# Two-layer decode attention: K scored in the step that transposes it, two more K slots kept, no self-waits on the tensor engine

## The chip, the core and the metric

The kernel runs on one core of a Trainium2 chip. The core has five engines that each work through a list of instructions in order: PE (matrix products), DVE (vector operations), ACT (activations and copies), POOL (here sums over partitions) and SP, which here only starts transfers (DMA). They meet at semaphores. The metric is the time of one execution in microseconds (us), as median of several runs.

## The reference

Two blocks, attention and a small feed-forward network, are applied twice to a batch of eight single tokens; both passes use the same caches and weights.

```python
B, Sq, D = 8, 1, 512;  Hq, Hkv, Sk, Dh = 32, 8, 8192, 128;  F = 1792     # bf16
def _A_ref(x, k_cache, v_cache, wq, wo):     # k_cache, v_cache [8, 8, 8192, 128]
    q = (x @ wq) split into 32 heads; four query heads share one K/V head
    p = _softmax(q @ k^T * Dh ** -0.5)
    return (p @ v, heads joined) @ wo
def _B_ref(x, w1, w2): return _silu(x @ w1) @ w2
x = x + _A_ref(_layernorm(x), ...);  x = x + _B_ref(_layernorm(x), ...)   # layer 0
x = x + _A_ref(_layernorm(x), ...);  x = x + _B_ref(_layernorm(x), ...)   # layer 1
```

K and V together are 268 MB, and both layers need all of them, so the kernel is mostly a stream of K and V into the core.

## The kernel before

**Tasks and positions.** A task is one K/V head of one batch row in one layer: 2 x 8 x 8 = 128 tasks. It has four granules (loads of 512 KB for K and as many for V), each of two halves; a half is a position, so a task has eight positions, whose number modulo 8 is called its phase here. Two positions, one granule, are called a step. The loop over `p` writes out the order of the work for every engine by hand.

**Slots.** Loads go into 27 slots of an arena. A K granule is transposed by PE (eight 128x128 transposes per half, `emit_t`, T below), and the result is copied from PSUM back to its own slot by ACT or DVE (ACT takes three copies of eight). Then `emit_s` (S) multiplies it with the queries: four products of 128x512 per granule. `emit_pv` (PV) multiplies V with the probabilities, `LP` = 14 positions later; eight products per half. `plan_loads` gives each load the slot that comes free earliest in planned order, and SP issues the loads in that order, each as soon as the last readers of its slot are done.

**Kept K.** Of the 32 K granules of a row the last `KEEP` = 18 stay in their slots, transposed, from layer 0 to layer 1: heads 4 to 7, and two of the four granules of head 3. Layer 1 then loads only V for them. `make_tasks` orders the tasks so that a row's kept heads run in layer 0, then a few tasks of other rows, then the same heads in layer 1 (the "kept tasks"). In the tasks between these two stretches, 27 - 18 = 9 slots are left for the stream.

**Order within a step.** `emit_t_until(p + LT)` with `LT` = 2 writes T one step ahead of S. At an odd `p` come S of this granule, then the PV of two halves, then at some phases a part of the softmax (`soft`: at phase 0 row maximum and spread on DVE; at 2 the shift, a small product on PE, then own and shift on DVE, then exp on ACT; at 4 a sum; at 5 the transposes of P and their copy on DVE; at 7 a reciprocal).

**Chains.** When a row's layer 0 attention is done, the small work that leads to its layer 1 query is cut into stages (`chain_of`), and one stage is written per position after the softmax part: residual sum ("attended"), three stages of a layer norm, two empty ones, two halves of w1, silu, an empty one, two halves of w2, a second norm of three stages, two empty ones, four quarters of wq. A norm's third stage is thirteen short DVE operations. For rows 1 to 6 the first norm's third stage falls on phase 2 of a task and the second's on phase 5; for rows 0 and 7 one position later. The chain ends just ahead of that row's kept tasks. Outside chains a head's share of the wo product (`add_heads`) is written at phase 7, as the output of a head gets ready.

**Waits.** `acquire` makes an engine wait for the last writer of all that an operation reads, and for the last writer and all readers of what it writes, its own earlier operations included.

Lines: copies 436 (ACT) and 438 (DVE), transposes 430, S 461, PV 534, shift 482, P transposes 510, projections 603, wo 621, norm 556 to 590; issues of loads 331.

Of the kernel before, what the change touches and what calls it, by code (L numbers as in the profile page):

```python
# [13 lines left out]
GPT = 8  # L14
GPG = 2
NSLOT = 27
KEEP = 18
LT = 2
PRE = 10
LP = 14  # L20
EARLY = 4
# [8 lines left out]
PVN = 12  # L30
CW = 32
SETTLE = 2
ACT_EVAC = (1, 4, 7)

BF16 = mybir.dt.bfloat16
FP32 = mybir.dt.float32
# [24 lines left out]
class Sync:  # L61
# [30 lines left out]
    def acquire(self, eng, reads=(), writes=()):  # L92
        toks = []
        for r in reads:
            if r.last_write is not None:
                toks.append(r.last_write)
        for r in writes:
            if r.last_write is not None:
                toks.append(r.last_write)
            toks.extend(r.reads)  # L100
        best = {}
        for t in toks:
            k = t.sem
            if k not in best or best[k].val < t.val:
                best[k] = t
        for t in best.values():
            self.wait(eng, t)

    def release(self, tok, reads=(), writes=()):
        for r in reads:  # L110
# [27 lines left out]
def make_tasks(nb, nkv, keep_from):  # L138


    first = int(keep_from)
    a = [[(0, b, g) for g in range(first)] for b in range(nb)]
    kept = [[(0, b, g) for g in range(first, nkv)] for b in range(nb)]
    c = [[(1, b, g) for g in range(first, nkv)] for b in range(nb)]
    d = [[(1, b, g) for g in range(first)] for b in range(nb)]
    ahead = [t for b in range(1, nb) for t in a[b]]
    behind = []
    tasks = a[0] + kept[0]
    na = 0
    for b in range(nb):  # L150
        if b:
            tasks += kept[b]
        size = -(-(2 * first * (nb - 1)) // nb) if b in (0, nb - 1) else 2 * first * (nb - 1) // nb
        must = max(0, first * min(b + 1, nb - 1) - na)
        nd = size if b == nb - 1 else min(len(behind), first, size - must)
        tasks += behind[:nd]
        del behind[:nd]
        take = ahead[na:na + size - nd]
        na += len(take)
        tasks += take  # L160
        if b + 1 == nb:
            tasks += behind
        tasks += c[b]
        behind += d[b]
    assert na == len(ahead)
    return tasks + d[nb - 1]


def plan_loads(tasks, kept, nslot, ngran):
# [3 lines left out]
    for i, (layer, b, g) in enumerate(tasks):  # L173
        for k in range(ngran):
            i0 = i * GPT + k * GPG
            if layer == 0 or (g, k) not in kept:
                need = -1 if i0 < PRE else i0 - LT
                last = i if layer or (g, k) not in kept else at[(1, b, g)]
# [28 lines left out]
def _build(ctx, nc, A_x, A_k_cache, A_v_cache, A_wq, A_wo, B_w1, B_w2, out):  # L207
# [12 lines left out]
    order = [(g, k) for g in range(HKV) for k in range(NGRAN)]  # L220
    kept = set(order[len(order) - KEEP:])
    tasks = make_tasks(B, HKV, (len(order) - KEEP) // NGRAN)
    assert len(tasks) == 2 * B * HKV
    task_at = {t: i for i, t in enumerate(tasks)}
    loads = plan_loads(tasks, kept, NSLOT, NGRAN)
    NG = len(tasks) * GPT
# [9 lines left out]
    def sb(shape, dt, name):  # L236
        _cnt[0] += 1
        return ctx.enter_context(nc.sbuf_tensor(f"{name}_{_cnt[0]}", shape, dt))
# [8 lines left out]
    def chunk(slot, c):  # L247
        o = slot * SLOT + c * 128
        return ARENA[:, o:o + 128]

    def half(slot, h):
        o = slot * SLOT + h * GRP * 128
        return ARENA[:, o:o + GRP * 128]
# [36 lines left out]
    own = sb([128, NQ * USED], FP32, "own")  # L290
# [23 lines left out]
    def r_half(slot, h):  # L314
        return res(f"slot{slot}_{h}")
# [19 lines left out]
    def mm_group(steps, reads=(), writes=()):  # L335
        def run():
            inst = None
            for f in steps:
                inst = f()
            return inst  # L340
        return op(pe, run, reads, writes)
# [14 lines left out]
    with nc.Block() as block:  # L356

        @block.sync
        def _(sync_eng):
# [47 lines left out]
            load_rest()  # L407

            evacs = [0]
            tevacs = [0]  # L410
            tnext = [0]

            def has_t(i):
# [3 lines left out]
            def where(i):  # L417
                _l, b, g = tasks[i // GPT]
                return b, g, (i % GPT) // GPG, i % GPG

            def emit_t(i):
                b, g, k, h = where(i)
                slot = k_slot[(b, g, k)]
                n = tevacs[0]
                tevacs[0] += 1
                tb = evacs[0] % NTP
                evacs[0] += 1
                tpv = TPp[tb][:, :].rearrange("p (k q) -> p k q", q=128)
                steps = [
                    lambda c=c: pe.transpose(tpv[:, c, :], chunk(slot, h * GRP + c), ident[:, :])  # L430
                    for c in range(GRP)
                ]
                mm_group(steps, reads=[r_half(slot, h), "ident"], writes=[f"TP{tb}"])
                dst = half(slot, h)
                if n % 8 in ACT_EVAC:
                    op(act, lambda: act.copy(dst, TPp[tb][:, :]), reads=[f"TP{tb}"], writes=[r_half(slot, h)])  # L436
                else:
                    op(dve, lambda: dve.tensor_copy(dst, TPp[tb][:, :]), reads=[f"TP{tb}"], writes=[r_half(slot, h)])  # L438

            def emit_t_until(i):  # L440
                while tnext[0] <= min(i, NG - 1):
                    if has_t(tnext[0]):
                        emit_t(tnext[0])
                    tnext[0] += 1
# [10 lines left out]
            def emit_s(i):  # L455
                ti = i // GPT
                b, g, k, _h = where(i)
                slot = k_slot[(b, g, k)]
                bank, qn = ti % NSCP, ti % NQB
                steps = [  # L460
                    lambda c=c: pe.matmul(  # L461
                        SCp[bank][c * QUAD:(c + 1) * QUAD, :], QB[qn][:, NGRAN - 1 - k:NGRAN - 1 - k + QUAD],
                        ARENA[:, slot * SLOT + c * KB:slot * SLOT + (c + 1) * KB],
                        start=(k == 0), stop=(k == NGRAN - 1),
                    )
                    for c in range(NQ)
                ]
                mm_group(steps, reads=[r_half(slot, 0), r_half(slot, 1), f"QB{qn}"], writes=[f"SC{bank}"])
# [230 lines left out]
            def add_heads(b):  # L699
                g = heads[b].pop(0)  # L700
                summed[b] += 1
                first, last = summed[b] == 1, summed[b] == HKV
                if b < B:
                    a = at1[b % 3]
                    wo_part(g, lambda h: a[:, h:h + 1], f"at1_{b % 3}", 1, first, last)
                else:
                    wo_part(g, lambda h: at2[:, h, :], "at2", B, first, last)
# [30 lines left out]
            for p in range(NG + LP + GPT + 1):  # L738
                tq = (p + LQ) // GPT
                if (p + LQ) % GPT == 0 and tq < ntask:  # L740
                    layer, b, _g = tasks[tq]
                    if layer == 1 and chain and chain_b[0] == b:
                        while chain:
                            chain.pop(0)()
                    emit_q(tq)
                emit_t_until(p + LT)
                if p % GPG == GPG - 1:
                    if p < NG:
                        emit_s(p)
                    for i in range(p - LP - GPG + 1, p - LP + 1):  # L750
                        if 0 <= i < NG:
                            emit_pv(i)
                ti, ph = p // GPT - 1, p % GPT
                if 0 <= ti < ntask and ph in soft:
                    for f in soft[ph]:
                        f(ti)
                if chain:
                    left = max(1, first1[chain_b[0]] - EARLY - p)
                    for _n in range(-(-len(chain) // left)):
                        chain.pop(0)()  # L760
                elif heads[turn[0]] and not (p < NG and tasks[p // GPT][0] and (tasks[p // GPT][2], 0) in kept
                                             and turn[0] < B):
                    add_heads(turn[0])
                done = p - LP - GPT
                if done >= 0 and done % GPT == 0 and done // GPT < ntask:
                    tj = done // GPT
                    emit_norm(tj)
                    layer, b, _g = tasks[tj]
                    if layer == 0:
                        heads[b].append(_g)  # L770
                    elif b == B - 1:
                        heads[B].append(_g)
                    if layer == 0 and tj == last0[b]:
                        assert not chain and turn[0] == b
                        chain.extend([lambda b=b: add_heads(b)] * (HKV - summed[b]) + chain_of(b))
                        chain_b[0] = b
                        turn[0] = b + 1
                issue_until(p)
# [48 lines left out]
```

## Time and profile before

| | |
|---|---|
| median of 3 runs | 1216.23 us (1215.27 to 1217.24) |
| profiled execution, its own time | 1213.55 us |
| span of its instructions | 1211.5 us |
| busy: PE, weight loads, DVE, ACT | 87%, 65%, 50%, 32% of the span |
| DMA | 473.51 MB on the load queue, 391 GB/s of reads over the span |
| loads of K, of V | 368, 512, each 512 KB |
| copies of transposed K: DVE, ACT | 460 of 688 ns, 276 of 1010 ns |

A line of a timeline gives start, duration, engine, source line, operation, output and inputs, count, and in brackets the idle time before it and what ended it. A line of windows gives the stretch, its length, then each engine's busy time, the granted PE clock, the DMA share and the rate. Ends of PE instructions are modelled, so PE is best read from start to start.

### The profile page before, as it was taken

Reading aid. Unit: us, or ns where it says so; the run is one execution under the profiler, and the core shown is the slowest. Engines: PE = TensorE matmul, PEld = TensorE weight load, DVE = VectorE, ACT = ScalarE, POOL = GpSimd, SP = SyncE. Lnnn points to the kernel's source line nnn. Section 1 sums busy time; section 2 is a strip of 40 time slices with the busy share of each in tenths; the row PEclk is TensorE's granted clock in tenths of the full one; section 3 lists DMA queues with packets and bytes.
Section 4 is the critical chain, followed back from the end, with each engine's and each line's share of the span. In section 5 each row is a group of like instructions: output and inputs, shape, how many; then the busy total and the mean of one; then the engine's idle time right before and its main releaser. Section 6 shows DMA issues by size and latency. Waiting matters only on the chain.

```text
span 1211.5 us, 46232 instructions
## 1 busy us (share of the span) xinstructions
PE 1049.8 (87%) x20216; PEld 793.0 (65%) x20216; DVE 609.6 (50%) x1853; ACT 385.4 (32%) x670; POOL 70.3 (6%) x172
## 2 busy tenths in 40 slices
PE   2698898888898899889888899889998899888985
PEld 2576775666666676667666676667666766667664
DVE  2454554546444554546454554546455554455453
ACT  1233332333233322333233332333233323333231
POOL 0000000000000000000000000000000000000000
PEclk9899999999999999999999999999999999999996
DMA  9999999999999999999999999999999999999994
GB/s 376 384 397 407 406 366 409 408 408 401 352 408 408 408 383 403 408 408 404 367 408 408 407 390 407 408 407 402 386 407 408 406 396 409 408 408 385 399 407 163
DMA packets 133927, 476.45 MB, mean 393 GB/s; under 512 B 14160, under 2 KB 20064, under 8 KB 133216
## 3 DMA queue, kind: packets, MB, share of 16 engines
q1 hardware_dynamic: 133728, 473.51, 99.1%
q8 instruction: 160, 2.62, 0.9%
q14 instruction: 39, 0.32, 0.1%
HBM read 473.44 MB, written 0.01 MB: 391 GB/s over the span
## 4 chain that ended last, share of the span: by engine, by line
DMA 46%; PE 38%; DVE 7%; SPq 5%; issue 3%; ACT 0%; POOL 0%; POOLq 0%; DVEq 0%
DMA arena<-in_A_k_cache_dram 43%; PE OTp L534 14%; PE TPp L430 10%; PE SCp L461 6%; SPq L331 5%; PE MISC L603 4%; DMA wo<-in_A_wo_dram 2%; DVE arena L438 2%; PE OTp L482 1%; DMA arena<-in_A_v_cache_dram 1%; PE TPp L510 1%; PE MISC L621 1%; DVE PT L514 1%; DVE rowmax L472 1%; DVE tr L586 1%
## 5 line engine op out<-in xcount | busy, mean ns | idle before, releaser
L438 DVE COPY arena<-TPp 128x1024 bf16<-128x1024 bf16 x460 | 316.3, 688 | 328.1 <-PE TPp L430 327.9
L430 PE MATMUL TPp<-ident,arena 128*128 128x128 bf16 x5888 | 417.0, 222 | 69.9 <-DMA arena<-in_A_k_cache_dram 54.0
L436 ACT COPY arena<-TPp 128x1024 bf16<-128x1024 bf16 x276 | 278.9, 1010 | 520.1 <-PE TPp L430 520.1
L534 PE MATMUL OTp<-PT,arena 128*128 128x48 bf16 x8192 | 383.1, 185 | 45.8 <-DMA arena<-in_A_v_cache_dram 6.7
L534 PEld LDWEIGHTS OTp<-PT,arena 128*128 128x128 bf16 x8192 | 273.8, 96 | 219.3 <-issue 87.5
L430 PEld LDWEIGHTS TPp<-ident,arena 128*128 128x128 bf16 x5888 | 345.9, 99 | 98.9 <-DMA arena<-in_A_k_cache_dram 79.4
L461 PE MATMUL SCp<-arena,QB 128*32 128x512 bf16 x2048 | 207.3, 394 | 8.5 <-DVE arena L438 5.0
L492 ACT ACTIVATE P<-SCp,shift 128x512 bf16<-128x512 f32 x128 | 88.2, 689 | 257.3 <-PE OTp L534 134.7
L501 POOL PARTITION_ALL_REDUCE ssa<-ssm x128 | 55.4, 433 | 998.6 <-DVE ssm L498 968.8
L461 PEld LDWEIGHTS SCp<-arena,QB 128*32 128x32 bf16 x2048 | 53.1, 93 | 58.4 <-DVE arena L438 6.4
L472 DVE TENSOR_REDUCE rowmax<-SCp 128x1 f32<-128x512 f32 x128 | 86.9, 679 | 0.0
L514 DVE COPY PT<-TPp 128x256 bf16<-128x256 bf16 x128 | 37.2, 291 | 86.6 <-PE TPp L510 86.6
L485 DVE SCALAR_TENSOR_TENSOR own<-OTp,real,far 128x64 f32<-128x64 f32 x128 | 35.9, 281 | 74.6 <-PE OTp L482 74.4
L482 PE MATMUL OTp<-spread,ones 128*128 128x64 f32 x256 | 51.2, 282 | 1.8 <-DVE spread L474 1.8
L621 PE MATMUL MISC<-at,wo 128*128 128x32 bf16 (+1 forms) x1152 | 40.5, 176 | 11.2 <-DMA wo<-in_A_wo_dram 7.7
L510 PE MATMUL TPp<-ident,P 128*128 128x128 bf16 x512 | 49.2, 218 | 0.0
L498 DVE TENSOR_SCALAR ssm<-hm,rs 128x4 f32<-128x4 f32 x128 | 28.5, 223 | 36.5 <-ACT P L492 36.5
L621 PEld LDWEIGHTS MISC<-at,wo 128*128 128x128 bf16 x1152 | 34.6, 96 | 11.8 <-DMA wo<-in_A_wo_dram 7.8
L482 PEld LDWEIGHTS OTp<-spread,ones 128*128 128x128 f32 x256 | 38.8, 192 | 3.0 <-DVE spread L474 3.0
L603 PE MATMUL MISC<-xnT,wq 128*128 128x32 bf16 (+1 forms) x1152 | 34.6, 176 | 4.5 <-issue 3.0
L603 PEld LDWEIGHTS MISC<-xnT,wq 128*128 128x128 bf16 x1152 | 32.3, 96 | 5.8 <-issue 3.3
L474 DVE TENSOR_SCALAR spread<-ident,rowmax 128x64 f32<-128x64 bf16 x128 | 32.6, 254 | 4.6
(47 smaller groups left out, 293.4 us busy)
## 6 DMA issues: line engine op xcount, KB each, us to landing
arena<-in_A_v_cache_dram SPq DMA_DIRECT2D x512, 512.0 KB, 10.2
arena<-in_A_k_cache_dram SPq DMA_DIRECT2D x368, 512.0 KB, 14.9
wq<-in_A_wq_dram SPq DMA_DIRECT2D x1, 4096.0 KB, 15.8
wo<-in_A_wo_dram SPq DMA_DIRECT2D x1, 4096.0 KB, 26.0
w<-in_B_w_dram SPq DMA_DIRECT2D x2, 1792.0 KB, 22.6
P<-in_A_x_dram SPq DMA_DIRECT2D x1, 8.0 KB
out_dram<-P SPq DMA_DIRECT2D x1, 8.0 KB
```

Of the source, the lines that this page charges most:

```text
L331: eng.dma_start(out_ap, in_ap).then_inc(counter.sem, 16)
L430: lambda c=c: pe.transpose(tpv[:, c, :], chunk(slot, h * GRP + c), ident[:, :])
L436: op(act, lambda: act.copy(dst, TPp[tb][:, :]), reads=[f"TP{tb}"], writes=[r_half(slot, h)])
L438: op(dve, lambda: dve.tensor_copy(dst, TPp[tb][:, :]), reads=[f"TP{tb}"], writes=[r_half(slot, h)])
L461: lambda c=c: pe.matmul(SCp[bank][c * QUAD:(c + 1) * QUAD, :], QB[qn][:, NGRAN - 1 - k:NGRAN - 1 - k + QUAD], ARENA[:, slot * SLOT + c * K ...
L472: op(dve, lambda: dve.tensor_reduce(rowmax[:, :], SCp[bank][:, :], AX.X, ALU.max), reads=[f"SC{bank}"], writes=["rowmax"])
L482: mm_group([lambda: pe.matmul(every, ones[:, :], spread[:, :], start=True, stop=True)], reads=["ones", "spread"], writes=[f"OT{ob}"])
L492: op(act, lambda: act.activation(P[:, :], SCp[bank][:, :], ACT.Exp, bias=shift[:, 0:1], scale=SM_SCALE, accum_out=rs[st][:, :]), reads=[f" ...
L510: lambda c=c: pe.transpose(tpv[:, c, :], P[:, c * 128:(c + 1) * 128], ident[:, :])
L534: lambda c=c, cc=cc: pe.matmul(otp, chunk(slot, h * GRP + c), pv[:, cc % CPB, cc // CPB % NQ, k, :].unsqueeze(2).to_broadcast([128, REP, P ...
L603: lambda o=o, k=k: pe.matmul(MISC[:, o * n:o * n + w], w_sb[:, k, o * 128:(o + 1) * 128], rhs_of(k).to_broadcast([128, w]) if n == 1 else ...
L621: lambda o=o, h=h: pe.matmul(MISC[:, o * w:(o + 1) * w], wo_sb[:, h, o * 128:(o + 1) * 128], rhs_of(h).to_broadcast([128, w]) if n == 1 el ...
```

## The change

`KEEP` goes from 18 to 20: five whole heads (3 to 7) keep their K, so 16 loads of K fewer are made, and seven slots are left to the stream between. The order of the tasks is the same. `LT` goes from 2 to 0, and S is written at the end of its step: a step is now T of half 0, T of half 1, PV of two halves, softmax part, chain stage or wo, S. Half 0 is always copied by ACT and half 1 by DVE. PE no longer waits for its own earlier operations.

```diff
-KEEP = 18
-LT = 2
+KEEP = 20
+LT = 0
-ACT_EVAC = (1, 4, 7)
...
+        own = self.eng_sem[self.nc.tensor.engine]
         for t in best.values():
-            self.wait(eng, t)
+            if t.sem is not own or eng is not self.nc.tensor:
+                self.wait(eng, t)
...
-                if n % 8 in ACT_EVAC:
+                if h == 0:
                     op(act, lambda: act.copy(dst, TPp[tb][:, :]), reads=[f"TP{tb}"], writes=[r_half(slot, h)])
                 else:
                     op(dve, lambda: dve.tensor_copy(dst, TPp[tb][:, :]), reads=[f"TP{tb}"], writes=[r_half(slot, h)])
...
                 emit_t_until(p + LT)
                 if p % GPG == GPG - 1:
-                    if p < NG:
-                        emit_s(p)
                     for i in range(p - LP - GPG + 1, p - LP + 1):
                         if 0 <= i < NG:
                             emit_pv(i)
...
                     add_heads(turn[0])
+                if p < NG and p % GPG == GPG - 1:
+                    emit_s(p)
                 done = p - LP - GPT
```

More of the change, by code (lines that the diff above doesn't have):

```diff
@@ L409, in _ @@
             evacs = [0]
-            tevacs = [0]
             tnext = [0]
@@ L423, in emit_t @@
                 slot = k_slot[(b, g, k)]
-                n = tevacs[0]
-                tevacs[0] += 1
                 tb = evacs[0] % NTP
```

## The prediction

> **What bounds the kernel now.** I read the page first: the DMA row, the GB/s in slices and the chain that ended last.
>
> ```profile
> span 1211.5 us, 46232 instructions
> GB/s 376 384 397 407 406 366 409 408 408 401 352 408 408 408 383 403 408 408 404 367 408 408 407 390 407 408 407 402 386 407 408 406 396 409 408 408 385 399 407 163
> DMA 46%; PE 38%; DVE 7%; SPq 5%; issue 3%; ACT 0%; POOL 0%; POOLq 0%; DVEq 0%
> ```
>
> The stream runs at a ceiling of 408 GB/s, with one dip in each eighth of the span. 473.5 MB at 408 GB/s are 1160 us; the last 18 us have no loads; the rest is start and dips. Windows laid around the flat part and around the dips of batch rows 1 to 6:
>
> ```profile
> 200.00:280.00 80.00, 69.27 (x1245) 51.78 (x1244) 38.81 (x101) 28.50 (x46) 3.44 (x8) 1.00 1.03 407
> ...
> 284.00:324.00 40.00, 35.15 (x794) 27.87 (x791) 21.71 (x80) 12.46 (x22) 2.54 (x6) 1.00 0.96 361
> 428.00:460.00 32.00, 29.99 (x670) 23.50 (x666) 17.70 (x59) 8.62 (x16) 2.10 (x5) 1.00 0.99 379
> 562.00:592.00 30.00, 26.37 (x580) 20.54 (x579) 15.79 (x55) 9.58 (x16) 2.09 (x5) 1.00 0.94 362
> 698.00:726.00 28.00, 26.23 (x583) 20.59 (x580) 16.56 (x56) 8.59 (x15) 2.10 (x5) 1.00 1.01 388
> 832.00:860.00 28.00, 25.33 (x553) 19.87 (x549) 14.35 (x52) 8.57 (x15) 2.10 (x5) 1.00 0.99 377
> 964.00:992.00 28.00, 26.11 (x586) 20.95 (x586) 16.19 (x53) 9.30 (x16) 1.68 (x5) 1.00 1.01 396
> ```
>
> The last number is GB/s. Length times (1 - GB/s / 408) gives the lost time: 4.6, 2.3, 3.4, 1.4, 2.1 and 0.8 us, mean 2.4. Each lies where a row's chain of small stages (norm, projections) is mixed into the last three tasks before that row's kept heads. In between the kernel is bound by loads, in the dips by the PE. The DMA view, asked for a flat stretch (404 to 424 us) and for a dip (444 to 452 us), gives the time from issue to landing:
>
> ```profile
> arena<-in_A_k_cache_dram SPq DMA_DIRECT2D x8, 512.0 KB, 8.5
> arena<-in_A_v_cache_dram SPq DMA_DIRECT2D x7, 512.0 KB, 9.0
> ...
> arena<-in_A_v_cache_dram SPq DMA_DIRECT2D x6, 512.0 KB, 5.6
> ```
>
> A load every 0.524 MB / 408 GB/s = 1.285 us; nine streaming slots make a cycle of 11.6 us, of which 8.75 are on the way and 2.8 are held by compute and the issue. When the PE falls late the 8.75 shrinks, and at 5.6 the rate has already fallen (352 GB/s): the cushion is about 3 us. Last, the timeline: PE and copies in a flat step, DVE in a chain, and an idle PE near the end.
>
> ```profile
> 379.13 1.07 PE L430 MATMUL TPp<-ident,arena 128*128 128x128 bf16 x16 [0.18 <-DMA arena<-in_A_k_cache_dram]
> 379.79 0.69 DVE L438 COPY arena<-TPp 128x1024 bf16<-128x1024 bf16 x1 [1.17 <-PE TPp L430]
> 380.13 0.40 PE L461 MATMUL SCp<-arena,QB 128*32 128x512 bf16 x4
> 380.24 1.01 ACT L436 COPY arena<-TPp 128x1024 bf16<-128x1024 bf16 x1 [1.20 <-PE TPp L430]
> 380.46 0.81 PE L534 MATMUL OTp<-PT,arena 128*128 128x48 bf16 x16
> ...
> 284.10 0.14 DVE L578 TENSOR_SCALAR vr<-s1a 128x1 f32<-128x1 f32 x1
> 286.39 0.18 DVE L590 TENSOR_TENSOR xnT<-xc,yr 128x4 bf16<-128x4 f32 x1
> 286.47 0.69 DVE L438 COPY arena<-TPp 128x1024 bf16<-128x1024 bf16 x1
> ...
> 1181.91 1.03 PE L430 MATMUL TPp<-ident,arena 128*128 128x128 bf16 x8 [1.52 <-DMA arena<-in_A_k_cache_dram]
> ```
>
> Start to start, a step (two positions) is T 1.00, S 0.33, PV 0.65: 1.98 us, under the 2.57 that its two loads take. The first copy starts 0.66 and the second 1.11 after the first transpose. The third stage of a norm holds DVE 2.47 us (284.10 to 286.57 with 11 operations between), and a copy waits behind it.
>
> **The change, part by part.** Sixteen K loads (two per row) and their 256 transposes go. The loads are on the path: 16 x 1.285 = **-20.6 us**. The PE's 16 x 1.00 us lie at the edge of the kept tasks, see below.
>
> *Fewer slots, scored sooner.* K was held over two steps: landing to the end of S in the next step, 2.57 + 1.00 + 0.40 = 4.0 us, V 0.75. Now K is held T 1.0, PV 0.5, S 0.4 and the wait for the copy: 2.4, V about 0.9, since V lands 1.285 after K and its slot is passed on with K's. The mean hold falls by 0.7 us, to 2.1; seven slots cycle in 9.0 us, so 6.9 are left on the way instead of 8.75: the cushion loses **1.9 us in each chain**. SP issues in order behind S, now the last PE group of the step; that is in the hold. Against it, the kept tasks now begin without transposes: two slots come free per 0.9 instead of 2.0 us, and the dip ends earlier, which I take at 0.9. Net +1.0 per chain.
>
> *Self-waits.* PV's second half waited for its first: the waits view has 512 such waits, 85.7 us, 0.17 each. PV becomes 0.48, I take 0.5. Other own waits were long done: 0.
>
> *S behind the copies.* Copy h1 (DVE) runs from 1.11 to 1.80 after the step's start; with 0.1 for the semaphore S starts at 1.9, where T and PV end at 1.5. A plain step is 1.9 + 0.33 = 2.23 us, still under 2.57; the four steps of a task with the shift, transposes of P and one head of wo come to about 9.4 against 8 x 1.285 = 10.3. Between chains this costs nothing; if this cover goes, each 0.1 above costs 0.1 per step. ACT gets 352 copies for 276, DVE 352 for 460; ACT's 76 x 1.01 = 77 us lie on an engine that is 32% busy.
>
> *DVE stages in a chain* were hidden by the transposes running a step ahead. Now they stand before copy h1 in the same step. In rows 1 to 6 the first third stage falls on phase 2 (even), behind the shift matmul: own and shift end at 1.5, the stage at 3.97, the copy at 4.64, S at 4.72: a step of 5.05 us. The second falls on phase 5, behind its own copy, and ends 2.5 us into the next step: 3.73. With 0.71 for half of w1 or w2, 0.81 for a quarter of wq, 0.22 for shift or P and 0.4 for a head, the eleven steps to the kept tasks take 5.05, 2.76, 2.9, 2.54, 3.13, 2.23, 3.73, 3.45, 3.67, 2.6, 2.23 = 34.3 us, 6.0 more than 11 x 2.57. To this come PE waits for nothing visible ("issue", 0.5 to 1.2 us each), some 1.4 per chain: 7.4 us late. Before, by the first S of each task, the three tasks ran 6.6, 4.1, 5.0, 3.5, 4.4 and 3.7 us over 3 x 10.28, mean 4.55 for a loss of 2.4. So lateness grows by 2.85 and the cushion shrinks by 1.0 net: **+3.85 per chain**, 6 x 3.85 = +23.1. In rows 0 and 7 the stages fall one position later (phases 3 and 6; steps of 3.45 and 3.95), I take +2.5 each: +5.0. Bounds: 0 if the cushion swallows it all; 5.0 per chain with no early end of the dip.
>
> *PE clock.* The 5.05 us step leaves the PE idle for 2.8 us. After the 1.52 us of idleness at 1181.9 eight transposes took 1.03 instead of 0.53 us, and the window 1181 to 1186 shows a granted clock of 0.66. Of the ten gaps between 1.0 and 1.7 us three were followed by such a slow stretch of some 3.4 us, which costs 1.7. 0.3 x 6 x 1.7 = **+3.1**; bounds 0 and 10. The Trainium skill (TensorE: Matmul & The Clock Gate, "What's actually happening") says that the clock halves after at least one idle window of about 3.4 us; no gap here would be that long, so by the rule this term would be 0 and the sum 3.1 lower. The trace already disagrees at 1.52 us, and its row decides.
>
> **Sum.** -20.6 + 23.1 + 5.0 + 3.1 = +10.6 on the span of 1211.5: 1222. The profiled execution took 1213.55, and the median shown is 1216.23, 2.7 above it; so the median goes to **1227**.
>
> **The rivals.** (1) *The cushion holds* (faster). Single loads issued into a drained queue landed in as little as 4.8 us (median of the dip at 312 to 318); if the rate holds down to 4 us, the cushion after is 2.9, and of 7.4 us of lateness 4.5 are lost, 2.1 more than before; 8 x 1.3 to 2.1 = 10 to 17 less 20.6: about 1209. It decides at a growth of 2.6 us per chain. For it: in the dip at 428 only 2.3 of 4.1 us were lost. Against: 352 GB/s at 5.6. The Trainium skill (DMA: Bandwidth & Descriptors, "Anatomy of one DMA") gives a fixed 2 us per DMA beside its bytes; by an estimate from that page the cushion would be larger still, which no flat stretch here can show. (2) *Plain steps no longer fit.* If S starts at 2.3 (semaphores, DVE's reductions ahead of the copy), a step with wo or shift passes 2.57 and the seven streaming tasks of each row lose 0.3 each: 8 x 7 x 0.3 = 17, 1244. For it: the margin is 0.9 us per task. Against: the seven slots' 6.9 us. (3) *No change that can be told*: the growth per chain is close to 2.6. (4) The clock gate closes in all six: 7 us more, 1234; inside my own case.
>
> **How the numbers follow.** Forecast with (4) 0.48, 1219 to 1237; rival 1 0.30, 1196 to 1213; rival 2 0.15, 1237 to 1255; rival 3 0.07. A measurement of this kernel can tell about 0.2%, 2.4 us. Faster 0.30, same 0.07, slower 0.63. The range leaves out a tenth at each end: 1202 to 1243; the likeliest case alone 1219 to 1237.
>
> **What the profile after would show.** Loads 352 for K; flat stretches still at 407 to 408; K and V land about 7 us after issue there. PE waits at S for DVE's copies some 0.3 us in plain steps and 2.8 us once in rows 1 to 6, with DVE in the norm's third stage; dips of 330 to 370 GB/s, 6 us lost each. The 512 PE-on-PE waits are gone. Wrong would be: dips no deeper than before (rival 1), or flat stretches under 400 (rival 2).

## The result, and the profile after

The changed kernel takes 1223.13 us (median of 6 runs, 1221.85 to 1225.82); the kernel before took 1216.74 beside it. The ratio is 1.0055, 95% interval 1.0039 to 1.0072: slower by about 6.4 us. The profiled execution took 1224.89 us, some 1.8 above its median.

From the profile of the kernel after: span, rate in slices, the chain that ended last, and the group of S (busy and mean of one, then idle time before it and what ended it). The last line is the same group in the kernel before.

```profile
span 1222.8 us, 45532 instructions
GB/s 372 385 397 407 396 344 409 408 399 371 367 408 408 384 328 410 408 402 363 376 407 407 369 366 409 408 406 344 379 408 405 366 349 408 408 406 349 391 407 177
DMA 57%; PE 23%; DVE 9%; SPq 5%; issue 4%; ACT 2%; POOL 0%; POOLq 0%; ACTq 0%; DVEq 0%
L459 PE MATMUL SCp<-arena,QB 128*32 128x512 bf16 x2048 | 208.8, 396 | 85.3 <-DVE arena L436 34.6 <-DVE rcp L519 17.6 <-DVE ssm L496 17.1
...
L461 PE MATMUL SCp<-arena,QB 128*32 128x512 bf16 x2048 | 207.3, 394 | 8.5 <-DVE arena L438 5.0
```

The ceiling is still 408 GB/s, 8.4 MB fewer are loaded, and the dips are deeper. The idle time before S was 8.5 us in the kernel before; it is 85.3 now, and the names shown behind it are all DVE operations. The windows after, over a flat part and the dips of rows 1 to 6, rate last:

```profile
200.00:280.00 80.00, 66.84 (x1248) 50.31 (x1249) 37.49 (x99) 35.67 (x53) 3.83 (x9) 1.00 1.02 405
...
280.00:320.00 40.00, 32.91 (x772) 28.13 (x772) 19.73 (x75) 14.42 (x24) 2.58 (x7) 0.96 0.96 347
416.00:460.00 44.00, 35.55 (x818) 29.81 (x814) 21.51 (x83) 14.42 (x24) 2.91 (x7) 0.96 0.94 340
552.00:592.00 40.00, 32.96 (x758) 27.87 (x756) 20.67 (x80) 15.11 (x25) 3.01 (x8) 0.96 0.97 347
688.00:728.00 40.00, 33.27 (x759) 27.99 (x756) 20.99 (x81) 15.17 (x25) 3.29 (x8) 0.96 0.95 346
828.00:872.00 44.00, 36.51 (x830) 29.68 (x830) 21.44 (x77) 13.59 (x24) 2.94 (x7) 0.96 0.94 343
964.00:1008.00 44.00, 36.03 (x828) 29.55 (x828) 21.62 (x79) 13.73 (x26) 2.94 (x7) 0.96 0.96 342
```

Against 408 GB/s these lose 6.0, 7.3, 6.0, 6.1, 7.0 and 7.1 us, mean 6.6 where it was 2.4: 25 us more. Rows 0 and 7 lose 4.3 and 4.6 where it was 3.0 and 2.3. Together +29 us against the -20.6 of the loads; the spans of the two profiled executions differ by 11.3, the medians by 6.4. In a second profiled execution of the changed kernel (`c1_after` below), over windows a little wider, rows 1 to 6 lose 5.8 on average.

The timeline of the kernel after, PE and then DVE, in row 1's chain:

```profile
280.62 0.62 PE L428 MATMUL TPp<-ident,arena 128*128 128x128 bf16 x8 [0.22 <-DMA arena<-in_A_k_cache_dram]
281.08 0.39 PE L480 MATMUL OTp<-spread,ones 128*128 128x64 f32 x2
281.30 0.61 PE L428 MATMUL TPp<-ident,arena 128*128 128x128 bf16 x8
281.90 0.57 PE L532 MATMUL OTp<-PT,arena 128*128 128x48 bf16 x16
285.17 0.62 PE L459 MATMUL SCp<-arena,QB 128*32 128x512 bf16 x4 [2.70 <-DVE ssm L496]
285.72 1.89 PE L428 MATMUL TPp<-ident,arena 128*128 128x128 bf16 x16
...
281.82 0.22 DVE L486 TENSOR_REDUCE shift<-own 128x1 f32<-128x64 f32 x1
281.96 0.14 DVE L576 TENSOR_SCALAR vr<-s1a 128x1 f32<-128x1 f32 x1
...
284.26 0.18 DVE L588 TENSOR_TENSOR xnT<-xc,yr 128x4 bf16<-128x4 f32 x1
284.34 0.69 DVE L436 COPY arena<-TPp 128x1024 bf16<-128x1024 bf16 x1
```

The second half is transposed by 281.9, but its copy waits for the norm's thirteen DVE operations and runs at 284.34. S waits 2.70 us (the label ssm is that of the DVE operation that ended last, just behind the copy), the step takes 5.10 us, and the next products are slow: S 0.62 instead of 0.40, sixteen transposes 1.89 instead of 1.07. Loads ahead of a chain, where the rate is still 402 GB/s, from issue to landing, 404 to 416 us:

```profile
arena<-in_A_k_cache_dram SPq DMA_DIRECT2D x5, 512.0 KB, 7.5
arena<-in_A_v_cache_dram SPq DMA_DIRECT2D x4, 512.0 KB, 6.9
```

### The profile page after: what moved, and what is told of

It reads as the page before. It is cut to its first block, busy times and chain, and to the rows that moved or that the text cites. A ratio compares the mean times of both kernels' runs of the same rounds, so it can differ in the third digit from the quotient of the medians.

```text
span 1222.8 us, 45532 instructions
## 1 busy us (share of the span) xinstructions
PE 990.2 (81%) x19960; PEld 769.0 (63%) x19960; DVE 563.3 (46%) x1745; ACT 462.2 (38%) x746; POOL 70.2 (6%) x172
## 4 chain that ended last, share of the span: by engine, by line
DMA 57%; PE 23%; DVE 9%; SPq 5%; issue 4%; ACT 2%; POOL 0%; POOLq 0%; ACTq 0%; DVEq 0%
DMA arena<-in_A_k_cache_dram 35%; DMA arena<-in_A_v_cache_dram 20%; PE TPp L428 10%; SPq L332 5%; PE MISC L601 4%; DVE arena L436 4%; PE SCp L459 4%; PE OTp L532 3%; DMA wo<-in_A_wo_dram 2%; ACT P L490 1%; PE OTp L480 1%; DVE tr L583 1%; DVE yr L586 1%; DVE tr L584 1%; DVE rowmax L470 1%
## 5 line engine op out<-in xcount | busy, mean ns | idle before, releaser
L434 ACT COPY arena<-TPp 128x1024 bf16<-128x1024 bf16 x352 | 356.2, 1012 | 571.7 <-PE TPp L428 571.7
L428 PE MATMUL TPp<-ident,arena 128*128 128x128 bf16 x5632 | 406.3, 224 | 45.1 <-DMA arena<-in_A_k_cache_dram 28.0
L428 PEld LDWEIGHTS TPp<-ident,arena 128*128 128x128 bf16 x5632 | 334.1, 101 | 141.4 <-DMA arena<-in_A_k_cache_dram 101.2
L436 DVE COPY arena<-TPp 128x1024 bf16<-128x1024 bf16 x352 | 242.5, 689 | 238.7 <-PE TPp L428 236.8
L532 PE MATMUL OTp<-PT,arena 128*128 128x48 bf16 x8192 | 296.5, 184 | 65.2 <-DMA arena<-in_A_v_cache_dram 55.4
L532 PEld LDWEIGHTS OTp<-PT,arena 128*128 128x128 bf16 x8192 | 250.0, 97 | 139.6 <-DMA arena<-in_A_v_cache_dram 123.1
L459 PE MATMUL SCp<-arena,QB 128*32 128x512 bf16 x2048 | 208.8, 396 | 85.3 <-DVE arena L436 34.6
L459 PEld LDWEIGHTS SCp<-arena,QB 128*32 128x32 bf16 x2048 | 59.5, 93 | 122.2 <-issue 55.3
```

The costliest lines, as they stand in the source:

```text
L459: lambda c=c: pe.matmul(SCp[bank][c * QUAD:(c + 1) * QUAD, :], QB[qn][:, NGRAN - 1 - k:NGRAN - 1 - k + QUAD], ARENA[:, slot * SLOT + c * K ...
L532: lambda c=c, cc=cc: pe.matmul(otp, chunk(slot, h * GRP + c), pv[:, cc % CPB, cc // CPB % NQ, k, :].unsqueeze(2).to_broadcast([128, REP, P ...
```

## The experiments

Ratios are to the kernel before, run beside it on the same chip. "Late" is by how much the three tasks ahead of the kept tasks of rows 1 to 6 run over 3 x 10.28 us, taken from the first S of each task and averaged: 4.6 us before, 5.9 after.

**The parts of the change, one by one.** First the self-waits alone, in the kernel before:

```diff
+        own = self.eng_sem[self.nc.tensor.engine]
         for t in best.values():
-            self.wait(eng, t)
+            if t.sem is not own or eng is not self.nc.tensor:
+                self.wait(eng, t)
```

> The kernel before with only this part of the change: the PE does not wait for its own earlier operations. Theory (flat stretches are bound by loads, only the dips by the PE): PV takes 0.5 us instead of 0.65 in some 12 steps of each of eight chains, 2 us per chain of the 2.4 lost: 12 to 16 us less, 1201 to 1205 us, flat stretches still at 407 to 408 GB/s. Rival (the waits lie beside other waits): 1216 us.

1211.3 us, ratio 0.9965 (0.9950 to 0.9980): faster by 4.3 us, a third of what theory said. PV did fall to 0.41 from start to start, but late only from 4.6 to 3.8. The timeline shows where a part went (the last line is one of the DMA queues of its page: packets, MB, share):

```profile
305.03 0.55 PE L605 MATMUL MISC<-xnT,wq 128*128 128x32 bf16 x16 [0.99 <-issue]
...
311.23 0.38 PE L512 MATMUL TPp<-ident,P 128*128 128x128 bf16 x4 [1.41 <-issue]
...
q8 instruction: 159, 2.61, 0.9%
```

The PE sits idle, once amid a group of products, and the profile names nothing that it waits for. In the same six windows these waits add up to 7.9 us in the kernel before and to 13.5 here: 0.9 per chain, nearly half of the 2 us that were to be saved. The traces point to a cause. The two waits end 1.45 and 1.33 us after a 16 KB load on the queue "instruction" has ended. Between 100 and 1180 us the thirteen kept traces hold 48 such waits of the PE over 0.8 us, and every one ends 1.2 to 1.6 us after the end of such a load, which is so at only 7% of all moments. So the PE probably waits here for its own instructions to be loaded; no run changes that, so it is not shown.

Then the slots alone:

```diff
-KEEP = 18
+KEEP = 20
```

> The kernel before with only this part: 20 kept granules, so seven streaming slots, with S still a step behind its transposes. Theory: 20.6 us of loads go; K is held 4.0 us, so of the 9.0 us of the slots' cycle some 6.2 are left on the way and the cushion loses 2.6 us per chain, 20.8, of which the earlier end of the dip gives back 7: 1209 to 1217 us. Rival (6.2 us on the way do not keep the load engines busy in the flat stretches near the chains): these fall under 400 GB/s and the time is 1220 us or more. Rival (a cushion is not needed): 1196 us.

1215.0 us, ratio 0.9990 (0.9975 to 1.0004). Loads worth 20.6 us went and nearly all came back. From 404 to 416 us loads take, from issue to landing:

```profile
arena<-in_A_k_cache_dram SPq DMA_DIRECT2D x5, 512.0 KB, 6.1
arena<-in_A_v_cache_dram SPq DMA_DIRECT2D x5, 512.0 KB, 6.6
```

This is no flat part, the rate is down to 371 GB/s. From 272 to 284 us it is 403 GB/s:

```profile
arena<-in_A_k_cache_dram SPq DMA_DIRECT2D x5, 512.0 KB, 6.7
arena<-in_A_v_cache_dram SPq DMA_DIRECT2D x4, 512.0 KB, 7.2
```

That is some 7 us against 8.75, so the shorter cycle of the slots leaves about 1.8 us less of cushion, much as in the changed kernel. Late even falls to 2.6, and the rate is lost all the same.

Both edits together, the old order kept:

> The kernel before with 20 kept granules and without the PE's self-waits; order of work, lookahead of the transposes and the choice of engine for the copies as before. Theory (the order inside a step is what costs): 20.6 us of loads go, 13 to 21 come back by the smaller cushion less its earlier end, 12 to 16 go with the waits: 1195 to 1205 us. Rival (seven slots with K held over two steps are the cause): 1216 us or more.

1205.53 us, ratio 0.9915 (0.9892 to 0.9938), half a microsecond above the range expected. So two of the three parts make the kernel faster by 10 us, and the third, the order inside a step, makes it slower by 1.0055 - 0.9915 = 1.4%, 17 us. In this third part are also `LT`, which moves loads in the plan, and the new split of the copies between ACT and DVE; no run takes these apart. The same with the self-waits put back in the changed kernel:

```diff
-            if t.sem is not own or eng is not self.nc.tensor:
-                self.wait(eng, t)
+            self.wait(eng, t)
```

> The changed kernel with the PE's waits for its own operations put back. Theory: in plain steps and in the 2.7 us wait they hide behind the copy that S waits for; in the seven steps of a chain where the PE has other work between PV and S they cost 0.17 each, 1.2 per chain: about 1232 us, 1228 to 1234. Rival (all of it lies behind S's wait): 1223 us.

1236.47 us, ratio 1.0173 (1.0154 to 1.0192): 13 us slower than the changed kernel, more than either theory said. Against b2, which has the same slots and waits in the old order, the order costs 1.8%, 22 us. The self-waits cost 4 us with nine slots and the old order, 9.5 with seven slots and the old order (b2 against b5) and 13 here. That fits a cushion that is used up, where each 0.17 us of delay is lost; this is a reading of the three differences.

**Is it the slots or the stall?** The changed kernel with nine streaming slots:

```diff
-KEEP = 20
+KEEP = 18
```

> The changed kernel with 18 kept granules, so nine streaming slots, and all else as changed. Theory (stages of a norm on DVE stand before the second copy, so S and the PE wait 2.7 us, then the PE clock is halved; the smaller cushion of loads on the way is only a part): the 5.1 us steps stay, 16 more loads cost 20.6 us, two more slots add 2.6 us of cushion to each of eight chains, 20.8: about 1223 us, between 1217 and 1229, and the dips still lose some 27 us in all. Rival (seven slots alone make the dips deeper): the dips are back at the 20 us of before, 1223 + 20.6 - 28 = 1216 us or less.

1226.57 us, ratio 1.0086 (1.0061 to 1.0112). The rival, that seven slots alone make the dips, is out: with nine of them the kernel is no faster. The two slots gave back some 17 of the 20.6 us that the 16 loads cost, 2.1 per chain: they have a price, but nine of them do not mend the dips. The windows show what they absorb, here row 1 of this kernel:

```profile
280.00:324.00 44.00, 36.52 (x841) 30.99 (x838) 22.64 (x84) 17.20 (x27) 3.31 (x8) 0.96 0.98 363
```

Rows 1 to 6 run 6.8 us late and lose 4.9, 4.3, 4.9, 5.1, 4.6 and 3.2 us, mean 4.5. So 2.3 us of lateness are absorbed with nine slots, as in the kernel before (4.6 late, 2.4 lost), and none with seven (5.9 late, 6.6 lost).

**Taking the stall away.** Both halves are transposed, and their copies written, ahead of the chain stage:

```diff
-                emit_t_until(p + LT)
+                emit_t_until(p | 1)
```

> The changed kernel with both halves of a granule transposed, and their copies written, at the even position, ahead of the softmax part and the chain stage of that position. Theory: the first norm's third stage in rows 1 to 6 now stands behind the copies, the 2.7 us of idle PE and the slow clock after it go: 6 x (2.7 + about 1) = 22 us, and some 2 us each in rows 0 and 7: about 1197 us, 1192 to 1204. Rival (the seven slots are the cause): the dips stay as deep, 1218 to 1223 us.

1209.96 us, ratio 0.9952 (0.9928 to 0.9976): 13 us below the changed kernel. The first norm's stall is gone, the rival with it. The second norm's got longer, as its timeline shows (PE, then DVE; the last line is the same S in the changed kernel):

```profile
297.73 0.56 PE L532 MATMUL OTp<-PT,arena 128*128 128x48 bf16 x16
300.71 0.62 PE L459 MATMUL SCp<-arena,QB 128*32 128x512 bf16 x4 [2.42 <-DVE rcp L519]
...
297.48 0.15 DVE L576 TENSOR_SCALAR vr<-s1a 128x1 f32<-128x1 f32 x1 [0.31 <-POOL s1a L571]
...
299.79 0.18 DVE L588 TENSOR_TENSOR xnT<-xc,yr 128x4 bf16<-128x4 f32 x1
299.87 0.69 DVE L436 COPY arena<-TPp 128x1024 bf16<-128x1024 bf16 x1
...
303.19 0.40 PE L459 MATMUL SCp<-arena,QB 128*32 128x512 bf16 x4 [1.48 <-DVE rcp L519]
```

That stage is written at phase 5, behind its own copies, and runs into the copy of the next step. It idled the PE some 1.47 us per row in the changed kernel and, in five of the six rows, 2.4 here. Over rows 1 to 6 that is 5 us of the 13 by which the expectation was missed; the rest is not traced.

The length of the stage, with nothing moved; a root is found in one step of Newton's method instead of three, so the computation itself changes:

```diff
-NEWTON = 3
+NEWTON = 1
```

> The changed kernel with one step of Newton's method for the root in a norm where there were three (a change of the computation): a third stage on DVE has 7 operations for 13, 1.16 us less. Theory (S waits for this stage): the PE idles 1.55 us instead of 2.7, and both stages of a chain are shorter by 1.16: rows 1 to 6 gain 2.2 each, 3.2 if the PE clock now stays up, rows 0 and 7 about 2 each: 17 to 23 us, 1200 to 1206 us. Rival (the length of the stages on DVE is hidden, the slots are the cause): 1221 to 1223 us.

1204.66 us, ratio 0.9908 (0.9886 to 0.9930): 18.5 us below the changed kernel, as theory said. PE in row 1's chain:

```profile
279.43 0.57 PE L532 MATMUL OTp<-PT,arena 128*128 128x48 bf16 x16
281.55 0.40 PE L459 MATMUL SCp<-arena,QB 128*32 128x512 bf16 x4 [1.54 <-DVE ssm L496]
281.88 1.07 PE L428 MATMUL TPp<-ident,arena 128*128 128x128 bf16 x16
```

The wait fell from 2.70 to 1.54, by the 1.16 us of the six operations, and the products behind it run at full speed. The kernel before has the same stages and mostly hid them, as S waited only 8.5 us there in all; no run shortens them in the old order.

**Both norms mended.** Halves together, and the third stage cut in two (`SETTLE` 1 for 2, so the chain keeps its length):

```diff
-                    for _n in range(NEWTON):
...
+                def third_a():
+                    third()
+                    newton(1)
+
+                def third_b():
+                    newton(NEWTON - 1)
...
-                return [first, second, third]
+                return [first, second, third_a, third_b]
```

> The changed kernel with both halves of a granule transposed and copied at the even position, and the norm's third stage cut in two stages (one step of Newton's method in the first, two in the second) in place of one of the two empty stages. Theory (S waits for stages on DVE that stand before the second copy): both stalls go, the 2.4 us that were left at the second norm too; 6 x 2.4 and some clock less than the 1210 us with the halves together alone: 1192 to 1200 us. Rival (what is left of the dips is the PE's own work and the seven slots): 1207 to 1211 us.

1205.81 us, ratio 0.9921 (0.9897 to 0.9945): better than both kernels, but only about 4 us under the version with the halves together, between theory and rival. Windows of the changed kernel's span (first) and of this one's, same stretch:

```profile
272.00:320.00 48.00, 39.70 (x913) 33.34 (x908) 24.23 (x88) 18.41 (x31) 3.41 (x9) 0.96 0.97 356
```

```profile
272.00:320.00 48.00, 42.47 (x986) 34.54 (x985) 25.66 (x98) 18.00 (x31) 4.21 (x10) 1.00 0.99 383
...
844.64 0.40 PE L459 MATMUL SCp<-arena,QB 128*32 128x512 bf16 x4 [2.47 <-issue]
```

Row 1's dip is mended (383 GB/s, late 2.3). Late is 2.5 and 2.2 in rows 2 and 6, but 4.1, 6.0 and 3.9 in rows 3 to 5, where the PE has more waits of the kind called "issue", here 2.47 us in row 5. This order, mended, gives what b5 gives without it (0.9921 and 0.9915); the earlier S brings nothing of its own that these runs can tell.

**The halved clock.** 64 products that nobody reads, at the place where the PE idles, rows 1 to 6:

```diff
+                def keep_warm():
+                    mm_group(
+                        [lambda k=k: pe.matmul(MISC[:, 0:CW], w1_sb[:, k % KT, 0:128],
+                                               ident[:, 0:CW], start=True, stop=True)
+                         for k in range(64)],
+                        reads=["w1", "ident"], writes=["MISC"])
...
                 def third():
+                    if warm:
+                        keep_warm()
```

> The changed kernel with 64 small matrix products, whose result nothing reads, ahead of the first norm's third stage in rows 1 to 6, where the PE would be idle; S waits for the same copy as before. If the halved PE clock after the idle stretch has a price of its own, it is gone: the first S, transposes and PV after the stretch took 2.9 us and would take 1.8, so 6 x 1.05 = 6 us less, about 1217 us (1214 to 1219). If the slow clock is hidden by later waits: 1223 us.

1222.12 us, ratio 1.0054 (1.0036 to 1.0071). Again, with more executions, beside the changed kernel:

> The changed kernel again, as the neighbour of the two that follow: 1223 us, 5 to 8 us over the kernel before.

> The kernel with 64 small matrix products ahead of the first norm's third stage in rows 1 to 6, again, beside the changed kernel on one chip. The windows around its dips lost some 5 us less in the first look, the medians differed by 1 us. If the halved clock has a price: 3 to 6 us below the changed kernel. If later waits hide it: within 2 us of it.

1222.81 us for the changed kernel (1.0059, 1.0042 to 1.0076) and 1219.44 with the products (1.0027, 1.0012 to 1.0042). Windows of the two over the same stretches, changed kernel first; the granted clock is the number before the last two:

```profile
276.00:320.00 44.00, 35.97 (x814) 30.64 (x813) 21.68 (x81) 15.59 (x23) 2.87 (x7) 0.92 0.93 345
412.00:456.00 44.00, 35.94 (x827) 30.61 (x824) 22.15 (x83) 16.70 (x25) 3.31 (x8) 0.96 0.95 350
...
686.00:730.00 44.00, 36.76 (x865) 30.62 (x864) 23.70 (x89) 16.46 (x26) 3.32 (x8) 1.00 0.98 365
```

```profile
276.00:320.00 44.00, 37.60 (x925) 32.05 (x922) 22.96 (x88) 16.46 (x26) 3.32 (x8) 1.00 0.98 366
412.00:456.00 44.00, 36.93 (x913) 31.49 (x910) 22.96 (x86) 16.46 (x26) 3.32 (x8) 1.00 0.96 352
```

With the products the clock is 1.00 in all six windows. Without them it halved in rows 1, 2, 3 and 5 of this execution and stayed up in rows 4 (the third line) and 6, though the PE idled 2.7 us in each of the six. The products are worth 3.4 us by this pair; in the run before it was 1 us by the medians and nothing by the ratios (1.0054 and 1.0055). The windows flatter the products, as their profiled execution is the fastest of its twelve. So the price is small and not settled more closely.

## Why the prediction was right

Direction and size came out: +10.6 us forecast, +6.4 measured, inside the range. Its terms, one by one:

- **Loads.** 352 K loads, as said, and 405 GB/s in the flat part (407 to 408 were said). No experiment times the 20.6 us alone; they follow from bytes and rate.
- **Cushion.** 6.9 us on the way were forecast; 7.5 and 6.9 are measured. But what the cushion absorbs was sized too large. Before, 4.6 us late lost 2.4; now 5.9 late lost 6.6, and in the second profiled execution 5.4 late lost 5.8. Nothing is absorbed any more, where the sum had let it absorb 1.2.
- **Lateness** was sized too large by about as much: 7.4 forecast, 5.9 and 5.4 in two profiled executions of the changed kernel. That these two errors cancel is luck: +3.85 lost per chain forecast, +4.2 and +3.4 measured. Rows 0 and 7 got +1.3 and +2.3 for 2.5 each.
- **DVE stages.** This was the mechanism. The step of 5.05 us is one of 5.10, the idle stretch of 2.8 us is 2.70, and shortening the stage or moving the copies ahead of it takes the time back (a4, a2, c3).
- **Self-waits.** The prediction only took PV at 0.5 us in its steps and gave the waits no term of their own; start to start PV came down to 0.41. The 2.0 us per chain stand in the expectation of b1, and there the count of 12 x 0.17 failed: alone the waits bring 4.3 us in all, 0.5 per chain, and nearly half of the 2.0 came back as PE waits called "issue".
- **S behind the copies** in plain steps is covered by the loads, as said: the flat part runs at 405 GB/s, with S waiting some 0.3 us.
- **PE clock.** +3.1 us were forecast as 0.3 of six events at 1.7 us. In the profiled execution it halved in the chains of all eight rows, for 3.4 us each; in the second one in six of eight, once for 6.8 us. The products that keep it up bring 0 to 3.4 us over six rows, up to 0.6 each. So the clock fell more often than was put and a fall cost less; that the sum stays in reach is luck too. By the Trainium skill (TensorE: Matmul & The Clock Gate, "What's actually happening") the clock falls after at least one idle window of about 3.4 us; the trace disagrees, since 2.6 to 2.7 us of idleness were enough in fourteen of sixteen chains of two profiled executions.

Rival 1, that the cushion holds, needed a growth of under 2.6 us per chain; it was 4.2 (3.4 in the second profiled execution). It had the rate hold until loads land in 4 us; in the dip at 450 to 456 us it was 301 GB/s with V loads at 6.7. Rival 2, plain steps over 2.57 us, would have shown under 400 GB/s in the flat part, which it does not.

## What to carry to other kernels

A lookahead hides more than the wait that it was made for: taking it out puts everything that another engine has queued ahead of the copy into the step, so list each engine's queue in that order before moving work. Where a stream of loads has few slots, first ask how much lateness the slots absorb: the same waits of 0.17 us were worth 4 us with nine slots and 9.5 to 13 with seven. Measure the parts of a combined change alone: here two were good for 10 us together, and the third took 17.

## What was not expected of the hardware

The PE clock halved, mostly for 3.4 us, after idle stretches of only 2.6 to 2.7 us, in eight of eight and six of eight chains of two profiled executions, and yet a fall cost no more than some 0.6 us. With its self-waits gone the PE has more waits for which the profile names nothing: 13.5 us against 7.9 in six windows of b1, up to 1.5 us at once there and 2.8 in c3. All 48 that are longer than 0.8 us end 1.2 to 1.6 us after a load of the instruction queue; that this load is what the PE waits for is likely, and not tested.
